# A decode kernel keeps part of a sixth record on chip between two rounds

## The chip, the cores and the metric

The kernel runs on one core of a Trainium2 chip. The metric is device time in microseconds (us), median of several runs. All data are 32-bit floats.

## What is computed

Four tokens (B = 4, D = 640) pass through two identical rounds. Each round is an attention over a cache and an MLP, both with a residual and a layer norm before them. The weights and the caches are the same in both rounds.

```python
# W = 1024 newest positions, Hq = 32 heads of Dh = 128, Dff = 1728
q = layernorm(x) @ wq                             # [4, 32, 128]
p = softmax(q . k_cache[:, :, -W:] * Dh ** -0.5)
x = x + (p . v_cache[:, :, -W:]) @ wo
h = relu(layernorm(x) @ w1)
x = x + h @ w2
# and all of it a second time
```

## The kernel before

**Records.** All that one head needs is packed in a record of 128 partitions by REC = 9,472 columns: the query weights (columns 0 to 640), K in two halves of 2,048 columns (640 to 4,736), V in two halves of 2,048 (4,736 to 8,832), and the output weights (8,832 to 9,472, from `WO`). A record is 4,736 KB. The MLP weights w1 (five chunks of FF = 1,728 columns) and w2 (54 tiles of FD = 160 columns) are 8,640 columns each. Per round, 32 records and both weights are read once; on-chip memory holds five whole records (`slot0` to `slot4`), a `ring` of 7,808 columns and, before the change, a tile `kept` of 1,152 columns.

**The order of the records.** Round zero goes through heads 0 to 31. The last five of them (27 to 31) stay in their slots, and round one begins with them, so that they are not loaded again; then it goes through 0 to 26. Of record 26, the last of round one, the columns from `KEPT` = 8,320 on stay in `kept` between the rounds.

**The loads.** All loads are in one list, `items`, written in the order in which they shall be issued. `pump()` walks the list strictly in order: it issues the first entry as soon as no column that it overwrites is `live`, and stops at the first that must wait. `done(key, lo, hi)` marks columns of a record as read and calls `pump()`. All loads are issued by SyncE (SP), in list order; at run time each waits for the readers of what it overwrites. Since one entry that must wait holds up all behind it, the list decides what the 16 DMA engines have queued.

**One head.** `query` multiplies the query weights by the normed input on PE (five matmuls into a PSUM tile, before the change `misc`), and DVE copies the result to `qT`. `scores` does 8 matmuls into one of two score tiles `sc_ps`, each of two PSUM banks. `softmax` takes the maximum on DVE and the exponentials on ACT in place. `weights` transposes them on DVE into `wT`. `values` does 8 matmuls into `o_ps`; `picks` and `output_T` bring the head's result into `oTs`, and `project` multiplies it by the output weights into `acc`. The heads are pipelined by hand: in iteration n of the main loop the scores of head n + 1, the values of head n and the query of head n + 2 are issued in this order.

**The end of a round.** The last three records are loaded in pieces (`ending`), so that the compute behind the last load is short. In round zero the output weights of the last five records come after them, then the MLP weights.

**The MLP of round zero.** At that time five slots hold records 27 to 31, so the 17,280 columns of MLP weights go through the ring (`MLP_RING`: name, size, first column in the ring). Before the change four chunks of w1 and five tiles of w2 fit at first; each later piece waits until the piece under it has been read. Behind the weights come the pieces of record 0 for round one, most of them into the ring too (`IN_RING`), the rest into the first slot that comes free (`IN_SLOT`). In round one the MLP weights go into slots that are free by then.

**Fillers.** `busy(n)` is a matmul whose result nobody reads; some are placed where PE would pause.

In the trace every operation stands at line 88 (L88), the helper `InOrder.call` that records them; the tiles' names tell them apart. The functions that the diff touches:

Of the kernel before, what the change touches and what calls it, by code (L numbers as in the profile page):

```python
# [32 lines left out]
F32 = mybir.dt.float32  # L33
AF = mybir.ActivationFunctionType
OP = mybir.AluOpType
# [3 lines left out]
P = 128  # L39
# [16 lines left out]
ENDS = 28  # L56
TILES[ENDS:ENDS] = [(13, 0), (13, 1)]
TCOLS = len(TILES) * FD
RING = 4 * FF + 896
KEPT = WO - 512  # L60

MLP_RING = [("w1", 1, 0), ("w1", 1, FF), ("w1", 1, 2 * FF), ("w1", 1, 3 * FF), ("w2", 5, 6912), ("w1", 1, 0),
            ("w2", 10, 1728), ("w2", 11, 3328), ("w2", 11, 5088), ("w2", 6, 6848), ("w2", 7, 0), ("w2", 4, 1120)]

IN_RING = [(256, 1664, 1760), (1664, 3200, 3168), (3200, 4736, 4704), (4736, 6272, 6240), (6272, 7296, 0),
           (7296, 7808, 1024)]

IN_SLOT = [(WO, REC, 0), (7808, WO, 640), (0, 256, 1664)]
W1_SLOT = [[0, 1], [2], [3], [4]]
W2_SLOT = [22, 20, 8, 4]  # L70
LATE = 5
# [24 lines left out]
def decode_kernel(ctx: ExitStack, tc: tile.TileContext, xf, rec, w1, w2, out):  # L96
# [5 lines left out]
    mean_of = sb.tile([P, P], F32, name="mean_of")  # L102
# [4 lines left out]
    x_sb = scratch[:, :FD]  # L107
    blocks = xT.rearrange("p (k j) -> p k j", j=32)[:, :, :B]
    spread = scratch[:, 256:288]
    hT = scratch.rearrange("p (m j) -> p m j", j=32)  # L110
# [12 lines left out]
    kept = sb.tile([P, REC - KEPT], F32, name="kept")  # L123
# [5 lines left out]
    misc = ps.tile([P, 512], F32, name="misc")  # L129
    outs = [o_ps, sc_ps[0][:, 512:]]  # L130

    dve.memset(x_sb, 0.0)
# [13 lines left out]
    dve.tensor_reduce(mean_of.rearrange("p (j s) -> p j s", j=NB), folded, op=OP.add, axis=AX.X)  # L146

    dve.tensor_reduce(of_block, mean_of[:, :16].rearrange("p (c j) -> p c j", j=4), op=OP.add, axis=AX.X)
    dve.tensor_reduce(pick, mean_of[:, :32].rearrange("p (c j) -> p j c", j=4), op=OP.add, axis=AX.X)
    dve.tensor_scalar(mean_of, mean_of, 1.0 / D, None, op0=OP.mult)  # L150
    dve.memset(small, EPS)
    dve.memset(eps_dh, EPS * DH)
    dve.memset(ones, 1.0)
# [1 line left out]
    for a in sc_ps:  # L155
        dve.memset(a, 0.0)

    order = [list(range(H)), list(range(H - NS, H)) + list(range(H - NS))]
    LAST = H - NS

    def home(h, r):

        return h % NS if not r or h >= LAST else (h - 6 + LAST) % NS

    items = []

    at = {("rec", 1, LAST - 1): [(KEPT, REC, "kept", 0)]}
    live = []
    buffers = dict(enumerate(slot)) | {"ring": ring, "kept": kept}

    def load(key, src, lo, hi, buf, col):
        items.append((key, src, lo, hi, buf, col))
# [16 lines left out]
    piece(0, hs[0], 0, V)  # L189
    piece(0, hs[0], V, REC)  # L190
    for h in hs[1:-3]:
        piece(0, h, 0, KEPT if h == LAST - 1 else WO if h >= H - LATE else REC)
        if h == LAST - 1:
            piece(0, h, KEPT, REC, "kept", 0)
    ending(0, hs, True)
    loaded = {"w1": 0, "w2": 0}
    for name, size, col in MLP_RING:
# [1 line left out]
        load((name, 0), {"w1": w1, "w2": w2}[name], n, loaded[name], "ring", col)  # L199


    hs = order[1]
    old = [home(h, 0) for h in hs[:NS]]
    new = hs[NS:]
    for lo, hi, col in IN_RING:
        piece(1, new[0], lo, hi, "ring", col)
    for lo, hi, col in IN_SLOT:
        piece(1, new[0], lo, hi, old[0], col)
    piece(1, new[1], K + VH, V, old[0], K + VH)
    piece(1, new[1], 0, K + VH, old[1], 0)  # L210
    piece(1, new[1], V, V + VH, old[1], K + VH)
    piece(1, new[1], V + VH, REC, old[0], V)
    for i in range(2, 6):
        piece(1, new[i], 0, V, *((old[i], 0) if i < 5 else ("ring", 0)))
        piece(1, new[i], V, REC, old[i - 1], V)
    for h in new[6:-3]:
        piece(1, h, 0, REC)
    ending(1, hs, False)
    for ks in W1_SLOT:
        load(("w1", 1), w1, ks[0] * FF, (ks[-1] + 1) * FF, home(LAST + 1, 0), ks[0] * FF)  # L220
    n = 0
    for size in W2_SLOT:
        load(("w2", 1), w2, n * FD, (n + size) * FD, home(LAST + 2, 0), n * FD)
        n += size

    def pump():

        while items:
            key, src, lo, hi, buf, col = items[0]
            if any(b == buf and x < col + hi - lo and col < y for b, x, y in live):  # L230
# [3 lines left out]
            at.setdefault(key, []).append((lo, hi, buf, col))  # L234
            items.pop(0)

    def pieces(key):
# [2 lines left out]
    def cols(key, lo, n):  # L240
# [3 lines left out]
                return buffers[buf][:, col + lo - x:col + lo - x + n]  # L244
        raise KeyError((key, lo, n))

    def done(key, lo, hi):

        if key[0] == "rec" and key[1] == 0 and key[2] >= LAST:
            return  # L250
        for x, y, buf, col in pieces(key):
            a, b = col + max(lo, x) - x, col + min(hi, y) - x
            if a < b:
                rest = []
                for bb, u, v in live:
                    if bb != buf or v <= a or b <= u:
                        rest.append((bb, u, v))
                    else:
                        rest += [(bb, p, q) for p, q in ((u, a), (b, v)) if p < q]
                live[:] = rest  # L260
        pump()


    def busy(n, to=sc_ps[1]):

        pe.matmul(to[0:1, :n], mean_of[:, 0:1], slot[home(LAST, 0)][:, K:K + n], start=True, stop=True)

    def center(fill):

        x = acc[:, :FD]  # L270
        dve.tensor_reduce(sums, x, op=OP.add, axis=AX.X)
        if fill:
            busy(256)
        pe.matmul(misc[:, :B], sums.to_broadcast([P, P]), pick, start=True, stop=True)
        dve.transpose(xT, x)
        dve.scalar_tensor_tensor(blocks, misc[:, :B].unsqueeze(1).to_broadcast([P, KB, B]), -1.0 / D, blocks,
                                 op0=OP.mult, op1=OP.add)
        dve.tensor_tensor(spread[:, :KB * B].rearrange("p (k b) -> p k b", b=B), blocks, blocks, op=OP.mult)
        dve.tensor_reduce(squares, spread[:, :KB * B].rearrange("p (k b) -> p b k", b=B), op=OP.add, axis=AX.X)
# [75 lines left out]
    def mlp(r):  # L355
# [39 lines left out]
    for r in range(2):  # L395
        hs = order[r]
        late = LATE if r == 0 else 2
        center(r > 0)
        query(r, hs[0])
        scores(r, hs[0], 0, True)  # L400
        softmax(0, True)
        query(r, hs[1])
# [71 lines left out]
```

## Time and profile before

| | |
|---|---|
| runs (us) | 718.20, 717.31, 719.21; median 718.2 |
| span of the profiled execution (first to last instruction) | 715.0 us; its own time was not listed beside it, only the three runs |
| busy share of the span | PE 73%, DVE 50%, PE weight loads 30%, ACT 13% |
| DMA | 303.90 MB, mean 425 GB/s |
| HBM | read 303.25 MB, written 0.08 MB |

The page has six parts: busy time by engine; the span in 40 slices, each digit a busy share in tenths; the DMA queues with their share of 16 engines' span; the chain of work that ended last, followed back from the last instruction; the costliest groups of instructions; and the DMA issues with the median time from issue to landing. A load lands when the last of the 16 DMA engines has finished its part. An issue early in its queue has a long time to landing without costing anything: the time is that of the loads ahead of it.

### The profile page before, as it was taken

The page shows a single profiled execution, that of the slowest core. Times are in us where ns is not written, and L with a number is a line of the kernel's source. Part 1 is how long each engine was busy: PE and PEld are TensorE (multiplying, and loading weights), DVE is VectorE, ACT ScalarE, POOL GpSimd, SP SyncE. Part 2 cuts the span into 40 slices and gives each one's busy share as a digit, 9 for nine tenths or more (in the row PEclk, how much of TensorE's full clock was granted, in tenths as well). Part 3 has the DMA queues.
Part 4 walks back from the last instruction along what each step waited for, and adds up shares of the span by engine and source line. Part 5 has one row for each costly group of instructions (what it writes and reads, how often), then busy time and mean ns, then how long its engine had stood idle before and what let it go on. Part 6 is the DMA issues. An engine that isn't in the chain of part 4 may idle for free.

```text
span 715.0 us, 8905 instructions
## 1 busy us (share of the span) xinstructions
PE 523.8 (73%) x3694; PEld 212.8 (30%) x3694; DVE 357.8 (50%) x1010; ACT 93.1 (13%) x145; POOL 1.1 (0%) x9
## 2 busy tenths in 40 slices
PE   4465868676677776759889898876877777586867
PEld 2131323322223231323224333332332323232323
DVE  3354535454444544446731777744444444455751
ACT  1201011010101101011110211201010110101201
POOL 0000000000000000000000000000000000000000
PEclk9678767668866868777999999957576677868989
DMA  9999999999999999999999999999999999999996
GB/s 374 439 438 433 422 435 435 439 432 420 438 440 433 425 429 439 427 428 429 426 415 390 426 426 433 441 430 427 435 441 429 433 425 438 437 429 422 432 423 290
DMA packets 15913, 303.90 MB, mean 425 GB/s; under 512 B 1777, under 2 KB 2049, under 8 KB 6145
## 3 DMA queue, kind: packets, MB, share of 16 engines
q1 hardware_dynamic: 15840, 303.32, 99.1%
q8 instruction: 29, 0.48, 0.2%
q14 instruction: 12, 0.09, 0.0%
q10 hardware_dynamic: 32, 0.01, 0.0%
HBM read 303.25 MB, written 0.08 MB: 424 GB/s over the span
## 4 chain that ended last, share of the span: by engine, by line
DMA 76%; PE 19%; DVE 4%; issue 1%; another core or an unknown queue 1%; ACT 0%
DMA slot<-rec 73%; PE sc_ps L88 7%; PE misc L88 5%; PE o_ps L88 4%; PE acc L88 3%; DMA ring<-w 3%; DVE scratch L88 2%; DVE small L88 1%; DVE oTs L88 1%; DVE t_ps L88 0%; ACT sc_ps L88 0%; DVE xT L88 0%; DVE qT L88 0%; DVE mrt L88 0%
## 5 line engine op out<-in xcount | busy, mean ns | idle before, releaser
L88 PE MATMUL misc<-xT,slot 128*128 128x4 f32 x624 | 103.3, 292 | 146.3 <-DMA slot<-rec 145.8
L88 PE MATMUL sc_ps<-slot,qT 128*4 128x512 f32 x992 | 199.0, 943 | 1.5 <-DVE qT L88 1.3
L88 PEld LDWEIGHTS misc<-xT,slot 128*128 128x128 f32 x624 | 97.7, 242 | 203.2 <-DMA slot<-rec 190.9
L88 ACT ACTIVATE sc_ps<-sc_ps,small 128x1024 f32<-128x1024 f32 (+1 forms) x68 | 76.7, 1127 | 552.2 <-DVE small L88 551.2
L88 PE MATMUL o_ps<-slot,scratch 128*16 128x512 f32 x978 | 137.5, 679 | 4.0 <-DVE scratch L88 2.6
L88 DVE TENSOR_REDUCE small<-sc_ps 128x1 f32<-128x1024 f32 x64 | 78.3, 1223 | 78.1 <-PE sc_ps L88 78.1
L88 DVE STREAM_TRANSPOSE t_ps<-sc_ps 128x512 f32<-128x512 f32 x128 | 93.2, 728 | 2.1
L88 DVE COPY qT<-misc 128x4 f32<-128x4 f32 x64 | 10.2, 160 | 158.1 <-PE misc L88 158.1
L88 PEld LDWEIGHTS o_ps<-slot,scratch 128*16 128x16 f32 x978 | 33.6, 119 | 132.8 <-issue 82.5
L88 DVE SCALAR_TENSOR_TENSOR scratch<-o_ps,of_block,scratch 128x128 f32<-128x128 f32 x186 | 65.2, 351 | 6.6
L88 PEld LDWEIGHTS sc_ps<-slot,qT 128*4 128x4 f32 x992 | 33.1, 115 | 83.8 <-issue 73.1
L88 PE MATMUL acc<-slot,oTs 128*4 128x160 f32 x496 | 36.9, 382 | 16.1 <-DVE oTs L88 15.6
L88 DVE TENSOR_SCALAR scratch<-o_ps,of_block 128x128 f32<-128x128 f32 x62 | 21.7, 350 | 35.4 <-PE o_ps L88 35.4
L88 PE MATMUL o_ps<-pick,scratch 128*128 128x4 f32 x124 | 28.8, 303 | 5.8 <-DVE scratch L88 5.8
L88 DVE TENSOR_TENSOR scratch<-t_ps,mrt 128x64 f32<-128x64 f32 x128 | 28.8, 225 | 4.7
L88 PEld LDWEIGHTS o_ps<-pick,scratch 128*128 128x128 f32 x124 | 25.8, 256 | 8.6 <-DVE scratch L88 8.6
L88 DVE COPY oTs<-o_ps 128x4 f32<-128x4 f32 x62 | 10.0, 162 | 14.1 <-PE o_ps L88 12.9
L88 PE MATMUL sc_ps<-slot,mean_of 128*1 128x512 f32 (+1 forms) x36 | 16.8, 558 | 0.0
L88 DVE TENSOR_SCALAR mrt<-of_batch,small 128x4 f32<-128x4 f32 x64 | 14.7, 230 | 2.2
L88 DVE STREAM_TRANSPOSE scratch<-small 128x32 f32<-128x32 f32 x64 | 12.9, 202 | 2.4 <-ACT sc_ps L88 2.4
L88 PEld LDWEIGHTS acc<-slot,oTs 128*4 128x4 f32 x496 | 6.8, 84 | 22.1 <-DVE oTs L88 20.8
L88 ACT ACTIVATION_READ_ACCUMULATOR sc_ps<-sc_ps,small 128x1 f32 x64 | 12.2, 191 | 0.0
(69 smaller groups left out, 119.4 us busy)
## 6 DMA issues: line engine op xcount, KB each, us to landing
slot<-rec SPq DMA_DIRECT2D x43, 4736.0 KB, 30.8
slot<-rec SPq DMA_DIRECT2D x17, 2368.0 KB, 18.8
slot<-rec SPq DMA_DIRECT2D x2, 4416.0 KB
slot<-rec SPq DMA_DIRECT2D x5, 1024.0 KB, 30.4
ring<-w SPq DMA_DIRECT2D x5, 864.0 KB, 10.8
slot<-rec SPq DMA_DIRECT2D x1, 4160.0 KB, 34.5
slot<-rec SPq DMA_DIRECT2D x2, 2048.0 KB, 42.0
slot<-rec SPq DMA_DIRECT2D x2, 1344.0 KB, 9.2
```

Source lines behind the costliest of these rows:

```text
L88: r = build(*args, **kwargs)
```

## The change

Record 26 (`SIXTH`) gets a home of its own, the ring, which grows from 7,808 to 9,152 columns; `kept` and `mean_of` go. In round zero it is loaded there as columns 0 to 9,152; its last 320 columns are loaded later over the first 320 of the ring, whose query weights have been read by then. After round zero has used the record, its columns from `HELD` = 5,024 on stay. The 320 columns and columns 5,024 to 5,216 are copied by DVE (`put_by`) into `hold`, a PSUM bank of 512 columns. That leaves the first `KEPT` = 5,216 columns of the ring for the MLP weights of round zero, and behind them for columns 0 to 5,024 of record 26, which are loaded again (`SIXTH_PIECES`). In round one record 26 comes sixth, after 27 to 31, and after its query DVE copies the 512 columns back (`put_back`). The other records of round one go whole into the slots, and w1 of round one goes into the ring.

To make a bank free, `misc` goes: queries are now written to the first four columns of the score tile that the same head's scores will fill next, and the small matmul of `center` to `o_ps`. Fillers take `ones` in place of `mean_of`, those in `values` write to `sc_ps[0]`, and in round one's MLP the three fillers behind the middle w1 chunks go.

```diff
-RING = 4 * FF + 896
-KEPT = WO - 512
-
-MLP_RING = [("w1", 1, 0), ("w1", 1, FF), ("w1", 1, 2 * FF), ("w1", 1, 3 * FF), ("w2", 5, 6912), ("w1", 1, 0),
-            ("w2", 10, 1728), ("w2", 11, 3328), ("w2", 11, 5088), ("w2", 6, 6848), ("w2", 7, 0), ("w2", 4, 1120)]
-
-IN_RING = [(256, 1664, 1760), (1664, 3200, 3168), (3200, 4736, 4704), (4736, 6272, 6240), (6272, 7296, 0),
-           (7296, 7808, 1024)]
-
-IN_SLOT = [(WO, REC, 0), (7808, WO, 640), (0, 256, 1664)]
+SIXTH = H - NS - 1
+RING = WO + 2 * FD
+KEPT = 3 * FF + 32
+HELD = KEPT - 192
+
+MLP_RING = [("w1", 1, 0), ("w1", 1, FF), ("w1", 1, 2 * FF), ("w1", 1, 0), ("w1", 1, FF), ("w2", 11, 2 * FF),
+            ("w2", 10, 0), ("w2", 10, FF), ("w2", 11, 2 * FF), ("w2", 10, 0), ("w2", 2, FF)]
+
+SIXTH_PIECES = [(2048, 2 * FF), (2 * FF, HELD), (0, FF), (FF, 2048)]
...
-    order = [list(range(H)), list(range(H - NS, H)) + list(range(H - NS))]
     LAST = H - NS
+    order = [list(range(H)), list(range(LAST, H)) + [SIXTH] + list(range(SIXTH))]
 
     def home(h, r):
 
-        return h % NS if not r or h >= LAST else (h - 6 + LAST) % NS
+        if h == SIXTH:
+            return "ring"
+        return h % NS if not r or h >= LAST else (h + LAST) % NS
...
-    at = {("rec", 1, LAST - 1): [(KEPT, REC, "kept", 0)]}
+    at = {("rec", 1, SIXTH): [(0, RING, "ring", 0), (RING, REC, "ring", 0)]}
...
-        last = WO if late else KEPT
-        for h, lo, hi in ((a, 0, V), (b, 0, V), (a, V, end), (c, 0, V), (b, V, end), (c, V, V + VH), (c, V + VH, last)):
+        for h, lo, hi in ((a, 0, V), (b, 0, V), (a, V, end), (c, 0, V), (b, V, end), (c, V, V + VH), (c, V + VH, end)):
...
-        piece(0, h, 0, KEPT if h == LAST - 1 else WO if h >= H - LATE else REC)
-        if h == LAST - 1:
-            piece(0, h, KEPT, REC, "kept", 0)
+        piece(0, h, 0, RING if h == SIXTH else WO if h >= H - LATE else REC)
+    piece(0, SIXTH, RING, REC, "ring", 0)
     ending(0, hs, True)
...
+    for lo, hi in SIXTH_PIECES:
+        load(None, rec[SIXTH], lo, hi, "ring", lo)
+    new = order[1][NS + 1:]
+    for i, lo, hi in ((0, 0, K), (0, K, K + VH), (0, K + VH, V), (1, 0, K + VH), (1, K + VH, V), (0, V, V + VH),
+                      (0, V + VH, REC), (2, 0, V), (1, V, REC), (3, 0, V), (2, V, REC), (4, 0, V), (3, V, REC),
+                      (4, V, REC)):
+        piece(1, new[i], lo, hi)
...
+    ending(1, new, False)
     for ks in W1_SLOT:
-        load(("w1", 1), w1, ks[0] * FF, (ks[-1] + 1) * FF, home(LAST + 1, 0), ks[0] * FF)
+        load(("w1", 1), w1, ks[0] * FF, (ks[-1] + 1) * FF, "ring", ks[0] * FF)
...
-        load(("w2", 1), w2, n * FD, (n + size) * FD, home(LAST + 2, 0), n * FD)
+        load(("w2", 1), w2, n * FD, (n + size) * FD, home(new[-5], 1), n * FD)
...
+        if key == ("rec", 0, SIXTH):
+            hi = min(hi, HELD)
...
+    held = [(0, 0, REC - RING), (REC - RING, HELD, KEPT)]
+
+    def put_by():
+
+        for col, a, b in held:
+            dve.tensor_copy(hold[:, col:col + b - a], ring[:, a:b])
+            free("ring", a, b)
+        pump()
+
+    def put_back():
+
+        for col, a, b in held:
...
+            dve.tensor_copy(ring[:, a:b], hold[:, col:col + b - a])
+            live.append(("ring", a, b))
...
-        pe.matmul(to[0:1, :n], mean_of[:, 0:1], slot[home(LAST, 0)][:, K:K + n], start=True, stop=True)
+        pe.matmul(to[0:1, :n], ones, slot[home(LAST, 0)][:, K:K + n], start=True, stop=True)
...
-    def query(r, h):
+    def query(r, h, s):
+        q = sc_ps[s][:, :B]
         key = ("rec", r, h)
         for k in range(KB):
-            pe.matmul(misc[:, 8:8 + B], cols(key, WQ + k * DH, DH), xblock(k), start=(k == 0), stop=(k == KB - 1))
+            pe.matmul(q, cols(key, WQ + k * DH, DH), xblock(k), start=(k == 0), stop=(k == KB - 1))
         done(key, WQ, K)
-        dve.tensor_copy(qT, misc[:, 8:8 + B])
+        dve.tensor_copy(qT, q)
...
-                busy(512, misc)
+                busy(512, sc_ps[0])
...
-            elif k < KB - 1:
+            elif r == 0 and k < KB - 1:
                 busy(512)
...
-            query(r, hs[n + 2])
+            query(r, hs[n + 2], n % 2)
...
+            if r == 0 and h == SIXTH:
+                put_by()
+            if r == 1 and hs[n + 2] == SIXTH:
+                put_back()
```

More of the change, by code (lines that the diff above doesn't have):

```diff
@@ L100, in decode_kernel @@
     ps = ctx.enter_context(tc.tile_pool(name="ps", bufs=1, space=PSUM))
-    mean_of = sb.tile([P, P], F32, name="mean_of")
     xT = sb.tile([P, FD], F32, name="xT")
@@ L107, in decode_kernel @@
     x_sb = scratch[:, :FD]
+    same = scratch[:, FD:FD + P]
     blocks = xT.rearrange("p (k j) -> p k j", j=32)[:, :, :B]
@@ L122, in decode_kernel @@
     ring = sb.tile([P, RING], F32, name="ring")
-    kept = sb.tile([P, REC - KEPT], F32, name="kept")
     sc_ps = [ps.tile([P, W], F32, name=f"sc_ps{i}") for i in range(2)]
@@ L128, in decode_kernel @@
     acc = ps.tile([P, 512], F32, name="acc")
-    misc = ps.tile([P, 512], F32, name="misc")
+    hold = ps.tile([P, 512], F32, name="hold")
     outs = [o_ps, sc_ps[0][:, 512:]]
@@ L145, in decode_kernel @@
     folded = ident.rearrange("p (j s) -> p s j", j=NB).unsqueeze(1).to_broadcast([P, NB, 32, NB])
[L146 to L150, printed above, removed]
+    dve.tensor_reduce(same.rearrange("p (j s) -> p j s", j=NB), folded, op=OP.add, axis=AX.X)
+    dve.tensor_reduce(of_block, same[:, :16].rearrange("p (c j) -> p c j", j=4), op=OP.add, axis=AX.X)
+    dve.tensor_reduce(pick, same[:, :32].rearrange("p (c j) -> p j c", j=4), op=OP.add, axis=AX.X)
     dve.memset(small, EPS)
@@ L156, in decode_kernel @@
         dve.memset(a, 0.0)
-    order = [list(range(H)), list(range(H - NS, H)) + list(range(H - NS))]
     LAST = H - NS
+    order = [list(range(H)), list(range(LAST, H)) + [SIXTH] + list(range(SIXTH))]
     def home(h, r):
-        return h % NS if not r or h >= LAST else (h - 6 + LAST) % NS
+        if h == SIXTH:
+            return "ring"
+        return h % NS if not r or h >= LAST else (h + LAST) % NS
     items = []
-    at = {("rec", 1, LAST - 1): [(KEPT, REC, "kept", 0)]}
+    at = {("rec", 1, SIXTH): [(0, RING, "ring", 0), (RING, REC, "ring", 0)]}
     live = []
-    buffers = dict(enumerate(slot)) | {"ring": ring, "kept": kept}
+    buffers = dict(enumerate(slot)) | {"ring": ring}
     def load(key, src, lo, hi, buf, col):
@@ L199, in decode_kernel @@
         load((name, 0), {"w1": w1, "w2": w2}[name], n, loaded[name], "ring", col)
[L202 to L216, printed above, removed]
+    for lo, hi in SIXTH_PIECES:
[5 more added lines that the diff above has]
+        piece(1, new[i], lo, hi)
+    for h in new[NS:-3]:
         piece(1, h, 0, REC)
-    ending(1, hs, False)
+    ending(1, new, False)
     for ks in W1_SLOT:
-        load(("w1", 1), w1, ks[0] * FF, (ks[-1] + 1) * FF, home(LAST + 1, 0), ks[0] * FF)
+        load(("w1", 1), w1, ks[0] * FF, (ks[-1] + 1) * FF, "ring", ks[0] * FF)
     n = 0
     for size in W2_SLOT:
-        load(("w2", 1), w2, n * FD, (n + size) * FD, home(LAST + 2, 0), n * FD)
+        load(("w2", 1), w2, n * FD, (n + size) * FD, home(new[-5], 1), n * FD)
         n += size
@@ L233, in pump @@
             live.append((buf, col, col + hi - lo))
-            at.setdefault(key, []).append((lo, hi, buf, col))
+            if key:
+                at.setdefault(key, []).append((lo, hi, buf, col))
             items.pop(0)
@@ L245, in cols, with free @@
         raise KeyError((key, lo, n))
+    def free(buf, a, b):
+        rest = []
+        for bb, u, v in live:
+            if bb != buf or v <= a or b <= u:
+                rest.append((bb, u, v))
+            else:
+                rest += [(bb, p, q) for p, q in ((u, a), (b, v)) if p < q]
+        live[:] = rest
     def done(key, lo, hi):
@@ L253, in done @@
             if a < b:
[L254 to L260, printed above, removed]
-        pump()
+                free(buf, a, b)
+        pump()
+    held = [(0, 0, REC - RING), (REC - RING, HELD, KEPT)]
[6 more added lines that the diff above has]
+        for col, a, b in held:
+            assert not any(buf == "ring" and x < b and a < y for buf, x, y in live), (a, b, live)
+            dve.tensor_copy(ring[:, a:b], hold[:, col:col + b - a])
+            live.append(("ring", a, b))
     def busy(n, to=sc_ps[1]):
-        pe.matmul(to[0:1, :n], mean_of[:, 0:1], slot[home(LAST, 0)][:, K:K + n], start=True, stop=True)
+        pe.matmul(to[0:1, :n], ones, slot[home(LAST, 0)][:, K:K + n], start=True, stop=True)
     def center(fill):
@@ L273, in center @@
             busy(256)
-        pe.matmul(misc[:, :B], sums.to_broadcast([P, P]), pick, start=True, stop=True)
+        pe.matmul(o_ps[:, :B], sums.to_broadcast([P, P]), pick, start=True, stop=True)
         dve.transpose(xT, x)
-        dve.scalar_tensor_tensor(blocks, misc[:, :B].unsqueeze(1).to_broadcast([P, KB, B]), -1.0 / D, blocks,
+        dve.scalar_tensor_tensor(blocks, o_ps[:, :B].unsqueeze(1).to_broadcast([P, KB, B]), -1.0 / D, blocks,
                                  op0=OP.mult, op1=OP.add)
@@ L398, in decode_kernel @@
         center(r > 0)
-        query(r, hs[0])
+        query(r, hs[0], 0)
         scores(r, hs[0], 0, True)
         softmax(0, True)
-        query(r, hs[1])
+        query(r, hs[1], 1)
         weights(0)
```

## The prediction

> **What bounds the kernel now.** I read the page first: span, the row of DMA tenths, the queues, the chain that ended last.
>
> ```profile
> span 715.0 us, 8905 instructions
> DMA  9999999999999999999999999999999999999996
> GB/s 374 439 438 433 422 435 435 439 432 420 438 440 433 425 429 439 427 428 429 426 415 390 426 426 433 441 430 427 435 441 429 433 425 438 437 429 422 432 423 290
> q1 hardware_dynamic: 15840, 303.32, 99.1%
> DMA 76%; PE 19%; DVE 4%; issue 1%; another core or an unknown queue 1%; ACT 0%
> ```
>
> Loads fill the 16 DMA engines for 99.1% of the span, from the first slice to the last but one. No slice is idle; the 22nd (375 to 393 us), where round zero's MLP runs out of the ring and round one begins, is the slowest of the inner ones at 390 GB/s. The chain says the same: 76% of it is a DMA.
>
> Then the windows view, for the rate of an undisturbed stretch and of that stage (columns: stretch, length, busy time and count on PE, PEld, DVE, ACT, POOL, granted clock, DMA share, GB/s), and the waits of a late stretch (446 to 680 us), for how far the compute is from binding:
>
> ```profile
> 374.00:388.00 14.00, 12.96 (x149) 5.58 (x141) 1.63 (x5) 1.08 (x3) 0.00 (x0) 1.00 0.99 380
> 500.00:650.00 150.00, 110.64 (x704) 46.15 (x708) 72.31 (x202) 16.85 (x26) 0.00 (x0) 0.72 1.00 432
> PE misc L88 <- DMA slot<-rec: 51.6, 18, 4.3
> ```
>
> Undisturbed, a load moves 432 GB/s. A column (128 partitions of four bytes) is 512 bytes, so 1,000 columns cost 1.185 us. PE waits for the next record 18 times, 2.9 us on average: up to that much extra compute in each record of this stretch is free.
>
> The end, from the chain and from SP's timeline (the third row holds the last two loads, issued at 689.07 and about 690.9), with the issue row of the last load (320 KB, 20.6 us from issue to landing):
>
> ```profile
> 681.02 2.30 PE misc L88 x10
> 707.75 4.26 PE acc L88 x112
> 712.03 0.33 DVE scratch L88
> 689.07 2.15 SPq L88 DMA_DIRECT2D slot<-w  x2
> slot<-w SPq DMA_DIRECT2D x1, 320.0 KB, 20.6
> ```
>
> The last weights land at 690.9 + 20.6 = 711.5, the last matmuls on them end at 712.0 and the copy out at 712.4. The compute that starts with the K half of the last record (681.0) arrives at that same moment. So two things tie at the end: the sum of all loads, and the 31 us of compute behind the last record's K half.
>
> **The bytes removed.** Before, round one loads 27 records less the 1,152 columns in `kept`: 27 x 9,472 - 1,152 = 254,592. After, it loads 26 records and, of record 26, only the 5,024 columns up to HELD: 26 x 9,472 + 5,024 = 251,296. Round zero and the weights are unchanged. That is 3,296 columns, 1.69 MB; at 1.185 us per 1,000 it is **-3.9 us** of a queue that never rests. Four issues fewer (105 against 109) I cost at nothing: SP's 0.33 us each lies beside the transfers.
>
> **The end still follows the loads.** After, the last record's tail is loaded whole, so 4,736 + 2,048 + 2,688 + 17,280 = 26,752 columns come behind its K half (the other half of the record before, its own two value pieces, the weights), where 25,600 did. The compute behind it therefore gets 1,152 columns, 1.4 us, more room, and three of round one's MLP fillers leave PE's queue, each at least as long as its pace in this timeline, 0.43 us (the second starts 0.43 us after the first; they come in two passes):
>
> ```profile
> 701.55 0.59 PE L88 MATMUL sc_ps<-slot,mean_of 128*1 128x512 f32 x1
> 701.98 0.59 PE L88 MATMUL sc_ps<-slot,mean_of 128*1 128x512 f32 x1
> ```
>
> Of the tie only the loads remain, and the 0.9 us from the last landing to the copy's end stays. So the compute adds nothing and takes nothing away: 0.
>
> **The smaller ring.** This is the price. The MLP weights of round zero went through 7,808 columns and now go through 5,216, that is 2,592 columns or 3.1 us less of loads queued ahead; behind them record 0 filled 7,552 columns and record 26 now fills 5,024, 3.0 us less. Is there that much to spare? SP's timeline gives three refill issues; the issue rows give their time to landing, each asked for by itself, and that of two later ones:
>
> ```profile
> 371.10 0.33 SPq L88 DMA_DIRECT2D ring<-w  x1
> ring<-w SPq DMA_DIRECT2D x1, 800.0 KB, 7.5
> 373.50 0.33 SPq L88 DMA_DIRECT2D ring<-w  x1
> ring<-w SPq DMA_DIRECT2D x1, 880.0 KB, 7.2
> 375.09 0.33 SPq L88 DMA_DIRECT2D ring<-w  x1
> ring<-w SPq DMA_DIRECT2D x1, 880.0 KB, 7.7
> 387.12 0.38 SPq L88 DMA_DIRECT2D ring<-rec  x1
> ring<-rec SPq DMA_DIRECT2D x1, 256.0 KB, 9.5
> ring<-w SPq DMA_DIRECT2D x1, 480.0 KB, 4.5
> ```
>
> First, the dip to 380 GB/s is not yet a stall of the path: the three land at 378.6, 380.7 and 382.8, 2.1 us apart for 880 KB, which is full rate. Landings follow the slowest of the 16 engines; only faster ones ran dry. Second, the spare: 7.2 to 7.7 us less 3.1 leaves 4.1 to 4.6 from issue to landing, of which the transfer takes 1.9 to 2.1. What is left, 2.2 to 2.5 us, must hold the fixed part of a load (issue, first byte, receipt). The trace never shows that part alone. It is at least nothing; at most, from the 480 KB row, 4.5 less 1.1 of transfer, 3.4 us; the nearest row is the output, 80 KB from the copy's end at 712.4 to the end of the span at 715.0, 2.6 us less 0.2 of transfer and with the program's end in it. I take 2.4.
>
> So refills fit to within 0.2 us, and what they miss counts once per turn of the ring: three chunks are 5,184 columns, 12,096 columns of weights and the 5,024 of record 26 are refilled, 3.3 turns. By 0 the cost is 0, by 2.4 it is 0 to 0.7 us, by 3.4 it is 1.2 x 3.3 = 4.0 us. I take **+0.3 us**.
>
> The Trainium skill, page "DMA: Bandwidth & Descriptors", section "Anatomy of one DMA — SWDGE (gpsimd) path", gives a load a fixed part of about 2.0 us beside its bytes, for another issuing engine than SP; by that figure every refill still fits, the cost is 0 and the time 714.3 us, as an estimate. No row here shows that part alone, so the sum keeps its own bounds.
>
> At the start of round one the ring's last piece landed at 387.12 + 9.5 = 396.6; 3.0 us earlier is 393.6. Then comes record 0's query part (640 columns, 0.8 us, released by the query of record 27) until 394.4, and then the first K half, released by these scores:
>
> ```profile
> 389.66 1.89 PE sc_ps L88 x8
> ```
>
> They end at 391.6; with 2.4 us the queue is fed at 394.0, 0.4 us in time; by 3.4 it is 0.6 us late. Cost 0, at worst 0.6.
>
> **The sixth record and SP's queue.** Record 26's last 320 columns wait for its own query (they overwrite it), and SP issues in order, so records 29 to 31 wait behind that. Whole records are issued far ahead:
>
> ```profile
> slot<-rec SPq DMA_DIRECT2D x43, 4736.0 KB, 30.8
> ```
>
> Of 30.8 us about 11.2 are the transfer, some 20 us are queue; 27 and 28 stand in it when the query of 26 runs, so this delay, about one record, is covered. If that cover were gone it would cost up to 11 us. The weights in the ring then wait for `put_by`, which runs in 26's own iteration, over two records ahead of their turn: 0.
>
> **The four copies.** DVE's rows by form:
>
> ```profile
> L88 DVE COPY qT<-misc 128x4 f32<-128x4 f32 x64 | 10.2, 160 | 158.1 <-PE misc L88 158.1
> L88 DVE COPY scratch<-acc 128x160 f32<-128x160 f32 x1 | 0.3, 326 | 3.9 <-PE acc L88 3.9
> ```
>
> From 160 ns for 4 columns and 326 for 160 comes 1.06 ns a column: 0.50 us for 320 columns, 0.36 for 192, 0.86 us for each of `put_by` and `put_back` (the rows copy out of PSUM, one of these goes into it; from nothing to twice that would change no conclusion). `put_by` stands before the next maximum on DVE, in a stretch where PE waits 2.9 us per record. `put_back` stands in the compute-bound start of round one and delays one record by 0.9 us; loads are then queued ahead, in `slot` pieces like this, issued at 424.9:
>
> ```profile
> slot<-rec SPq DMA_DIRECT2D x1, 2368.0 KB, 19.1
> ```
>
> 19.1 us with 5.6 of transfer: 13 us ahead. Less the 3 us and the 0.9 it remains fed. 0.
>
> **`misc` gives up its bank.** Queries now write the first four columns of the score tile that is next to be filled. Its old scores were read by the transposes of the iteration before, and `values`, ahead of the query on PE, already waits for these. New scores there already wait for the copy to `qT`. So no wait is added; were one, up to 2.9 us a record would be hidden. `mean_of` for `ones` in the fillers changes no shape. 0.
>
> **Sum.** -3.9 + 0.3 = -3.6 us: the profiled 715.0 becomes 711.4. The runs' median, 718.2, lies 3.2 above the profiled span, for launch and end, which stay: **714.6 us**. About 0.3%, 2.2 us, is what this kernel's measurement tells from no change (three runs span 717.3 to 719.2).
>
> **Rivals.** *Starved refills.* The fixed part is nearer 3.4 us, and the ring turns 3.3 times with 1.2 us of waiting each, perhaps half of that: 1.5 to 4 us of the gain go, 716 to 718. For it: the margin is near 0, and the stage's dip shows that some engines already run dry. Against: landings kept full pace.
> *Slower: PE at half clock through the weights.* The trace grants half clock in places; here a w1 chunk lasts longer than at full clock:
>
> ```profile
> 367.54 0.91 PE sc_ps L88 x8
> 369.41 1.62 PE L88 MATMUL sc_ps<-ring,xT 128*4 128x432 f32 x8 [0.65 <-DMA ring<-w]
> 370.81 1.06 PE L88 MATMUL sc_ps<-slot,mean_of 128*1 128x512 f32 x1
> ```
>
> If all five chunks fall into such a stretch, each with such a filler behind it, a chunk costs 2.7 us where its load takes 2.05: 3.2 us late, and with it the refills, up to 4.0: -3.9 + 7.2 = +3.3, 721 us. It decides from 6.1 us lost on. Against: the stretch from 374 to 388 had a clock of 1.00.
> *No fewer bytes on the path:* the end is compute after all and the loads saved become idle time. Time 718.2. Against: the compute behind the last K half starts 4,448 columns, 5.3 us, earlier.
>
> **How the numbers follow.** Forecast 0.70 (713.0 to 716.0, faster). Starved refills 0.19 (0.08 still faster by over 0.3%, 0.11 within it). Half clock with starved refills 0.07, slower. Bytes off the path 0.04, within. Faster 0.78, within 0.3% 0.15, slower 0.07. The range: below, no stall and a scatter of a microsecond as the runs show, 713.0; above, half of the starved case, 717.0; what lies outside is the slower rival and the rest of the starved one and of the fourth, under 0.2.
>
> **What would show it.** q1 moves 1.69 MB less, 301.6 MB; its share stays at about 99%; the stretch from 366 to 396 us shows refills with 4 to 5 us from issue to landing and no landing gap over the transfer; the last w2 lands 3 to 4 us earlier and the copy out 0.9 us behind it. Wrong would be: DMA share visibly under 0.9 between 368 and 396; SP waiting for the query of 26 with an empty queue behind it; a PE wait for w2 at the end longer than before.

## The result and the profile after

The change makes no difference that can be measured: 718.55 us (median of 12 runs) against 718.38 before, a ratio of 1.0006 with a 95% interval from 0.9991 to 1.0022. Measured a second time, on another chip, it was 1.0006 [0.9985, 1.0026]. The forecast was 714.6.

The page of the kernel after (span, DMA share and GB/s in 40 slices of 17.9 us, the load queue, the chain that ended last):

```profile
span 717.1 us, 8939 instructions
DMA  9999999999999999999989999999999999999996
GB/s 377 435 435 434 435 428 430 436 434 433 430 430 434 435 432 435 431 427 424 424 345 333 409 434 428 444 425 434 436 433 436 422 431 436 438 434 418 429 426 286
q1 hardware_dynamic: 15264, 301.64, 98.6%
DMA 80%; PE 15%; DVE 3%; issue 1%; another core or an unknown queue 0%; DVEq 0%; SPq 0%
```

The bytes went as planned: 303.32 MB became 301.64. Yet the span is longer, and the queue's share fell from 99.1% to 98.6%. Most of that stands in two slices, the 21st and 22nd (359 to 394 us), with 345 and 333 GB/s where before had 415 and 390. The windows view of the last head of round zero (354 to 361) and of the MLP with the start of round one (366 to 398); columns as in the prediction, the last three are granted clock, DMA share and GB/s. Before, then after:

```profile
354.00:361.00 7.00, 5.25 (x39) 0.89 (x32) 5.61 (x14) 1.30 (x2) 0.00 (x0) 1.00 0.99 411
366.00:398.00 32.00, 27.55 (x235) 10.83 (x234) 6.89 (x28) 5.73 (x10) 0.00 (x0) 0.89 1.01 400
```

```profile
354.00:361.00 7.00, 6.06 (x36) 1.02 (x25) 5.25 (x14) 1.29 (x2) 0.00 (x0) 0.52 0.99 412
366.00:398.00 32.00, 24.75 (x240) 9.52 (x240) 5.67 (x23) 4.44 (x8) 0.00 (x0) 0.96 0.90 324
```

In 32 us the change moves 76 GB/s less, 2.43 MB; at 432 GB/s that is 5.6 us, more than the 3.9 us of bytes that it saves. The waits of 366 to 400 us name who stands still (engine, tile, releaser: us in total, times, longest). Before, then after:

```profile
PEld sc_ps L88 <- DMA ring<-w: 2.4, 2, 1.7
PE sc_ps L88 <- DMA ring<-w: 2.4, 3, 1.0
PEld acc L88 <- DMA ring<-w: 0.5, 1, 0.5
```

```profile
PEld acc L87 <- DMA ring<-w: 6.4, 4, 2.1
PEld sc_ps L87 <- DMA ring<-w: 5.6, 3, 3.4
PE sc_ps L87 <- DMA ring<-w: 3.0, 2, 2.5
PE acc L87 <- DMA ring<-w: 2.7, 4, 1.2
```

PE now waits for the ring all through the MLP. The timeline of after shows the loop, PE's reads and SP's issues (SP's third row is the first slot that comes free in round one):

```profile
368.68 0.91 PE L87 MATMUL sc_ps<-ring,xT 128*4 128x432 f32 x8 [0.80 <-DVE sc_ps L87]
369.65 16.14 SPq L87 DMA_DIRECT2D ring<-w  x8
...
375.68 0.91 PE L87 MATMUL sc_ps<-ring,xT 128*4 128x432 f32 x8 [2.51 <-DMA ring<-w]
377.94 0.91 PE L87 MATMUL sc_ps<-ring,xT 128*4 128x432 f32 x8 [0.52 <-DMA ring<-w]
...
382.79 0.99 PE L87 MATMUL acc<-ring,scratch 128*4 128x160 f32 x20 [0.79 <-DMA ring<-w]
386.04 5.72 SPq L87 DMA_DIRECT2D ring<-rec  x4
388.01 0.86 PE L87 MATMUL acc<-ring,scratch 128*4 128x160 f32 x19 [1.18 <-DMA ring<-w]
393.44 3.51 SPq L87 DMA_DIRECT2D slot<-rec  x3
```

The first chunk is read from 368.68 to 369.6, and only then, at 369.65, can the first refill be issued. The three chunks that the ring holds have all landed by 371.3 in the trace. The refill is read at 375.68, 6.0 us after its issue; at full pace it would have landed 2.05 us (its transfer) behind the third chunk, at 373.3. The DMA slices of 366 to 400 us (0.85 us each) show the hole; before, then after:

```profile
DMA  9999999999999989989999999999999999999999
```

```profile
DMA  9755396999999999979999989999989958989999
```

There are two holes: at 367 to 372, and at 392 to 394, where the first pieces of record 26 come. The end itself is as before, with the copy out right behind the last matmuls on the last weights (713.64, waiting for the DMA):

```profile
713.64 0.11 PEld L87 LDWEIGHTS acc<-slot,scratch 128*4 128x4 f32 x8 [0.35 <-DMA slot<-w]
714.16 0.33 DVE L87 COPY scratch<-acc 128x160 f32<-128x160 f32 x1 [4.29 <-PE acc L87]
```

### The profile page after: what moved, and what is told of

Its sections match the earlier page's. It is cut to its first block, busy times and chain, and to the rows that moved or that the text cites. A ratio compares the mean times of both kernels' runs of the same rounds, so it can differ in the third digit from the quotient of the medians.

```text
span 717.1 us, 8939 instructions
## 1 busy us (share of the span) xinstructions
PE 516.8 (72%) x3686; PEld 208.9 (29%) x3686; DVE 359.1 (50%) x1013; ACT 93.0 (13%) x145; POOL 1.1 (0%) x9
## 3 DMA queue, kind: packets, MB, share of 16 engines
q1 hardware_dynamic: 15264, 301.64, 98.6%
## 4 chain that ended last, share of the span: by engine, by line
DMA 80%; PE 15%; DVE 3%; issue 1%; another core or an unknown queue 0%; DVEq 0%; SPq 0%
DMA slot<-rec 68%; PE sc_ps L87 8%; DMA ring<-rec 6%; PE o_ps L87 4%; DMA slot<-w 3%; PE acc L87 3%; DMA ring<-w 3%; DVE scratch L87 2%; DVE oTs L87 1%; DVE small L87 0%; DVE t_ps L87 0%; DVE ring L87 0%; DVE mrt L87 0%; DVE xT L87 0%
## 5 line engine op out<-in xcount | busy, mean ns | idle before, releaser
L87 PE MATMUL sc_ps<-xT,slot 128*128 128x4 f32 x620 | 99.5, 287 | 148.9 <-DMA slot<-rec 146.6
L87 PEld LDWEIGHTS sc_ps<-xT,slot 128*128 128x128 f32 x620 | 95.4, 238 | 203.7 <-issue 194.0
L87 PE MATMUL o_ps<-slot,scratch 128*16 128x512 f32 x960 | 132.9, 674 | 2.5 <-DVE scratch L87 1.6
L87 DVE COPY qT<-sc_ps 128x4 f32<-128x4 f32 x64 | 10.2, 160 | 160.9 <-PE sc_ps L87 160.9
L87 PE MATMUL sc_ps<-slot,small 128*1 128x512 f32 (+1 forms) x36 | 17.1, 568 | 0.0
L87 DVE COPY oTs<-o_ps 128x4 f32<-128x4 f32 x62 | 10.0, 162 | 14.0 <-PE o_ps L87 12.9
L87 DVE STREAM_TRANSPOSE scratch<-small 128x32 f32<-128x32 f32 x64 | 12.9, 202 | 1.6 <-ACT sc_ps L87 1.6
L87 PE MATMUL sc_ps<-ring,xT 128*4 128x432 f32 x80 | 10.0, 605 | 4.6 <-DMA ring<-w 3.0
```

The lines of the kernel that those rows point to most:

```text
L87: r = build(*args, **kwargs)
```

## The experiments

**Theories.** A: what runs ahead is too short. The ring's free part fell from 7,808 to 5,216 columns, and at two places, the start of the MLP and the start of round one, the queue runs dry while SP waits for PE; that gives back what the bytes save. B: the delay of PE, which worked at half clock in the last head, is what costs, whatever the ring. T: the end of the kernel gains or loses something that the prediction put at nothing.

**The yardstick.** Two quantities are worked out from every trace. The loss in the MLP is the time from the landing of the first w1 chunk of round zero to that of the last w2 piece, less the columns that land between, at 1.185 us per 1,000. The loss at the start of round one is the same from there to the landing of the first half record that is loaded in one piece (2,368 KB, at some 415 to 427 us).

**1. Four chunks in the ring.** Part of record 26 is given back to the loads: 1,728 columns more to load than the change, 1,568 fewer than before.

```diff
-KEPT = 3 * FF + 32
+KEPT = 4 * FF + 32
...
+MLP_RING = [("w1", 1, 0), ("w1", 1, FF), ("w1", 1, 2 * FF), ("w1", 1, 3 * FF), ("w1", 1, 0), ("w2", 10, FF),
+            ("w2", 10, 2 * FF), ("w2", 11, 3 * FF), ("w2", 10, 0), ("w2", 10, FF), ("w2", 3, 2 * FF)]
...
+SIXTH_PIECES = [(2 * FF + 480, 3 * FF), (3 * FF, HELD), (0, FF), (FF, 2 * FF), (2 * FF, 2 * FF + 480)]
```

> The change with a ring of 6,944 columns for the weights (four chunks, not three) and so 6,752 columns of record 26 loaded again (not 5,024). Theory A, the ring is too shallow: what the change saves in bytes it loses again while the DMA engines run dry at the start of round zero's MLP and at the start of round one; 1,728 columns more depth cover 2.0 us of each gap, 1,728 columns more to load cost 2.0 us once, so the net is a gain over the change: 717.2 to 718.0, 0.3 to 1.0 us under the kernel before. Theory B, the loss comes from another part of the change (queries in the score banks, fillers, copies): the depth does nothing and the bytes cost 2.0 us, 720 to 721.

Measured: 714.79 us, 0.9957 [0.9942, 0.9971]: faster than both kernels, by more than was expected. The stage is whole again:

```profile
366.00:398.00 32.00, 27.05 (x232) 9.75 (x232) 6.42 (x26) 5.73 (x10) 0.00 (x0) 0.89 1.01 397
```

**2. Four chunks, without reloading the extra part.** Bytes as in the change, ring as in experiment 1; columns 5,024 to 6,752 of record 26 are not loaded again (the edit is against experiment 1).

```diff
-SIXTH_PIECES = [(2 * FF + 480, 3 * FF), (3 * FF, HELD), (0, FF), (FF, 2 * FF), (2 * FF, 2 * FF + 480)]
+SIXTH_PIECES = [(2 * FF + 480, 5024), (0, FF), (FF, 2 * FF), (2 * FF, 2 * FF + 480)]
```

> As four_chunks, but columns 5,024 to 6,752 of record 26 are not loaded again (left out), so that it loads as many bytes as the change with a ring one chunk deeper in the MLP; the depth at the start of round one is that of the change. Theory A: the gap at the start of the MLP closes, 2 to 3 us; the gap at the start of round one stays: 715.5 to 716.5. Theory B: no difference from the change, 718 to 719.

Measured: 715.63 us, 0.9963 [0.9946, 0.998]. With the change's bytes and one chunk more of ring the time is 2.9 us better than the change: that is the hole in the MLP (loss 0.6 us where the change has 4.7). But 2.05 us of loads fewer than in experiment 1 make nothing faster: at the start of round one the loss is 4.3 us, against 2.0 there. The bytes left out there only make the second hole longer.

**3 and 4. 3.2 us of DVE work that PE waits for**, before round zero's MLP, in the kernel before and in the change.

```diff
+        if r == 0:
+            for _ in range(4):
+                dve.transpose(t_ps, sc_ps[1][:, 512:])
+            dve.tensor_copy(xT, xT)
```

> The kernel before with 3.2 us of DVE work between round zero's last norm and its MLP, so that the ring is read 3.2 us later. Theory A: the old ring holds 7.1 us of loads behind the first chunk and lets DMA run on; 0.5 to 1.5 us slower. Theory B (depth does not matter, loads are late for another reason): as much slower as late_after is against the change.

> The change with the same 3.2 us of DVE work before round zero's MLP. Theory A: its ring is already empty when the MLP starts, so that the whole delay comes through: 3.0 to 3.3 us slower than the change, about 721.7. Theory B: the same cost as in late_before.

Measured: 721.35 us, 1.0052 [1.0032, 1.0073], and 722.75 us, 1.0057 [1.0039, 1.0075]. The second is 3.7 to 4.2 us over the change, somewhat more than expected; the first, 3.0 to 3.7 us over before, is a miss for A, as the old ring pays the delay nearly as the new one does. In both traces the delay is longer than the DVE work: PE came out of it with a clock of 0.50 and read the first chunk in 1.62 us instead of 0.91, so that the first refill was issued 4.4 and 4.2 us later than in the traces of before and of the change. How much of that the old ring could take is read from the trace of before. Its first refill is issued alone, by the end of the first chunk's matmuls,

```profile
368.51 0.33 SPq L88 DMA_DIRECT2D ring<-w  x1
```

and what was queued lands at 374.5, so that the refill's place at full pace is at 374.5 + 2.05 = 376.55. The delayed change shows what a load takes on an empty queue; its DMA slices and GB/s from 366 to 400 us, then SP's issue and PE's read of that load:

```profile
DMA  9854300000869999958999999999999899898999
GB/s 407 342 236 195 138 41 0 0 0 0 114 252 407 390 376 407 238 207 331 375 395 414 444 384 380 383 389 429 379 361 256 348 415 267 325 359 322 380 407 389
```

```profile
373.81 4.14 SPq L87 DMA_DIRECT2D ring<-w  x3
378.35 0.11 PEld L87 LDWEIGHTS sc_ps<-ring,xT 128*4 128x4 f32 x8 [0.88 <-DMA ring<-w]
```

Nothing moves from 371.1 to 374.5; 864 KB issued at 373.81 are read at 378.35, 4.5 us later, of which 2.05 are the transfer. So before's first refill would arrive at 368.51 + 4.5 = 373.0 on an empty queue, 3.5 us ahead of its place. The delay of 4.4 us goes past that by 0.9, and the refill of the delayed kernel landed 1.0 us behind its place. The rest of its loss in the MLP, 4.9 us in all, comes with the later refills, which start from there. (Its profile, 725.8 us, is its slowest run.)

**5. The fillers alone**: the kernel before without the three fillers of round one's MLP.

```diff
-            elif k < KB - 1:
+            elif r == 0 and k < KB - 1:
```

> The kernel before without the three fillers of round one's MLP, the one edit of the change that touches the compute behind the last load. Theory T (in the kernel before, compute and loads tie at the end, and where half clock falls on the last MLP the compute ends later): 0.5 to 1.3 us faster, 717.1 to 717.9. Theory L (the end follows the loads alone): no difference.

Measured: 717.11 us, 0.9993 [0.9981, 1.0006]. The interval holds the gain that T forecast and none at all; not resolved.

**6. The banks alone**: the kernel before with queries in the score banks, `center` on `o_ps` and `ones` in the fillers.

```diff
...
-            pe.matmul(misc[:, 8:8 + B], cols(key, WQ + k * DH, DH), xblock(k), start=(k == 0), stop=(k == KB - 1))
+            pe.matmul(q, cols(key, WQ + k * DH, DH), xblock(k), start=(k == 0), stop=(k == KB - 1))
...
```

> The kernel before with the queries written into the score banks, center's matmul into o_ps and fillers from ones, the ring and the loads as they were. If these edits are free, as predicted: within 0.15% of the kernel before. If a shared bank adds a wait that loads do not hide: slower by over 0.3%, which would then be part of what the change lost.

Measured: 717.37 us, 1.0001 [0.9986, 1.0017]: free, to within 0.2%. Its profile shows something else. Windows of 700 to 709 us, before and then this kernel, and this kernel's end:

```profile
700.00:709.00 9.00, 9.00 (x95) 3.25 (x88) 1.35 (x5) 2.65 (x5) 0.00 (x0) 1.00 0.93 392
```

```profile
700.00:709.00 9.00, 9.00 (x48) 2.04 (x49) 0.48 (x3) 1.58 (x2) 0.00 (x0) 0.69 0.87 367
```

```profile
710.43 4.07 PE L88 MATMUL acc<-slot,scratch 128*4 128x160 f32 x112
...
714.59 0.33 DVE L88 COPY scratch<-acc 128x160 f32<-128x160 f32 x1 [3.47 <-PE acc L88]
```

The last load lands at 711.44 in the trace, as before (711.5), yet the copy out comes at 714.59 instead of 712.03: here the compute ends 2.6 us late. PE had a clock of 0.69 in round one's MLP, where before had 1.00; that this is the whole reason was not tested. Of the other traces with the old end, those of before and of experiment 5 don't show it, that of experiment 3 does (2.4 us). In all ten traces of kernels with the sixth record the copy is 0.56 or 0.57 us behind the last landing.

**7. Two chunks**, the dose upward: 1,728 columns fewer to load than the change, one chunk less of ring.

```diff
-KEPT = 3 * FF + 32
+KEPT = 2 * FF + 32
...
+MLP_RING = [("w1", 1, 0), ("w1", 1, FF), ("w1", 1, 0), ("w1", 1, FF), ("w1", 1, 0), ("w2", 11, FF),
+            ("w2", 10, 0), ("w2", 11, FF), ("w2", 10, 0), ("w2", 11, FF), ("w2", 1, 0)]
...
+SIXTH_PIECES = [(160, FF), (FF, HELD), (0, 160)]
```

> The change with a ring of 3,488 columns for the weights (two chunks) and 3,296 columns of record 26 loaded again: 1,728 columns (2.0 us) fewer to load than in the change, and as many fewer ahead. Theory A, depth: in both gaps DMA runs dry 2.0 us sooner, and each refill of the weights waits for a whole turn, some 4.5 us for a chunk on an empty queue and 1 us to read it, for two chunks 5.5 us against 4.1 of transfer: 722 to 728. Bytes alone: 716.5.

Measured: 724.32 us (4 runs), 1.0087 [1.0061, 1.0114], as A has it. Fewer bytes, more time:

```profile
366.00:398.00 32.00, 20.52 (x192) 7.86 (x196) 3.40 (x16) 2.66 (x5) 0.00 (x0) 0.95 0.85 287
```

**8. Four chunks with the three fillers of round one's MLP**, as before the change (the edit is against experiment 1).

```diff
-            elif r == 0 and k < KB - 1:
+            elif k < KB - 1:
```

> four_chunks with the three fillers of round one's MLP put back. Theory T, with the longer stretch of loads behind the last K half still giving 1.4 us of room: 0 to 0.7 us slower than four_chunks, 714.8 to 715.5. If the fillers were all of the extra gain: 716.

Measured: 715.56 us, 0.9964 [0.9949, 0.998]; against 0.9957 and 0.9950 without them the intervals overlap. Fillers are not what made experiment 1 better than expected.

**9 and 10. The change and four chunks again**, on one chip.

> The change once more, unedited, beside the others on one chip and for a second profile. The first profile read the first weight chunk 2.5 us after it landed, 1.4 us later than before, since PE had half clock in the last head of round zero. If the loss is the depth of the ring, it comes without that too: ratio to the kernel before within 0.998 to 1.003, and again 2 us or more lost by landings between the third and fourth chunk or later refills. If it was that stretch of half clock, this profile, if free of it, shows 2 to 4 us less span.

> four_chunks once more, unedited, beside the change on one chip. Theory A: 0.994 to 0.997 of the kernel before, so that four chunks are 2 to 4 us faster than three.

Measured: 719.40 us, 1.0006 [0.9985, 1.0026], and 715.58 us, 0.9950 [0.9931, 0.9969]. The change's second profile has the same stage:

```profile
366.00:398.00 32.00, 25.80 (x238) 9.46 (x237) 5.14 (x21) 4.44 (x8) 0.00 (x0) 0.90 0.92 338
```

**11. The change, with its held part loaded again too**: 3,936 columns, 4.7 us of transfer, right behind the pieces of record 26.

```diff
-SIXTH_PIECES = [(2048, 2 * FF), (2 * FF, HELD), (0, FF), (FF, 2048)]
+SIXTH_PIECES = [(2048, 2 * FF), (2 * FF, HELD), (0, FF), (FF, 2048), (KEPT, RING)]
...
+        free("ring", KEPT, RING)
```

> The change, but columns 5,216 to 9,152 of record 26, which stand in the ring all the time, are loaded again behind the other pieces of record 26: 3,936 columns, 4.7 us, more to load, and so much more queued at the start of round one; the MLP's ring is as in the change. If the gap at the start of round one is real (2 to 2.5 us) that part comes back: 2 to 3 us slower than the change, 720.5 to 721.5. If only the MLP's gap exists: 4.7 us slower, 723.

Measured: 721.50 us, 1.0040 [1.0023, 1.0057]. Of 4.7 us of transfer only 0.34%, 2.4 us, appear in the time. The other 2.2 us (by the medians of 9 and 11, 2.6) fill time in which the change's queue stands idle. In the traces a part of that is at the start of round one: from the landing of the ring's last piece of record 26 to that of the first half record, the change loses another 0.9 and 3.3 us, this kernel 0.6. The rest may lie in the MLP, where this trace lost less than those of the change, for a reason that comes below.

**12. Five chunks**: 160 columns more to load than before, a ring 864 columns larger.

```diff
-KEPT = 3 * FF + 32
+KEPT = 5 * FF + 32
...
+MLP_RING = [("w1", 1, 0), ("w1", 1, FF), ("w1", 1, 2 * FF), ("w1", 1, 3 * FF), ("w1", 1, 4 * FF), ("w2", 10, 0),
+            ("w2", 10, FF), ("w2", 10, 2 * FF), ("w2", 10, 3 * FF), ("w2", 11, 4 * FF), ("w2", 3, 0)]
...
+SIXTH_PIECES = [(480, FF), (FF, 2 * FF), (2 * FF, 3 * FF), (3 * FF, 4 * FF), (4 * FF, HELD), (0, 480)]
```

> The change with a ring of 8,672 columns for the weights (all of w1 at once) and 8,480 columns of record 26 loaded again, 160 columns more bytes than the kernel before. Theory A: no gap is left to close, so against four_chunks only the bytes count, 1,728 columns, 2.0 us slower: 716.5 to 717.5, four chunks being next to the best. If depth still pays at four: at or below four_chunks, 715.

Measured: 716.53 us, 0.9977 [0.9963, 0.9991]. All 12 runs lie between 716.47 and 716.78; those of before and of the change spread over 4 us and more, those of four chunks over 2. In the stage:

```profile
366.00:398.00 32.00, 27.89 (x250) 9.64 (x248) 9.12 (x31) 5.73 (x10) 0.00 (x0) 0.95 1.02 421
```

This run closes the account. With five chunks hardly anything starves, so its 716.5 us less 1.185 us per 1,000 columns is what a kernel would take by its bytes; what its profiled execution took beyond that should be its losses beyond those of five chunks (0.3 in the MLP and 1.3 behind it). A time is longer than the span of its execution by 2.0 us for before (median of its 92 later runs, 1.7 to 2.2) and by 1.7 for kernels with the sixth record, so that before's profiled execution took about 717.0. All in us:

| kernel | ring | by bytes | profiled execution | beyond | loss MLP | loss start | sum less 1.6 |
|---|---|---|---|---|---|---|---|
| five chunks | 8,672 | 716.5 | 716.5 | 0 | 0.3 | 1.3 | 0 |
| before | 7,808 | 716.3 | 717.0 (715.0 + 2.0) | 0.7 | 0.4 | 1.6 | 0.4 |
| before, no fillers | 7,808 | 716.3 | 718.8 | 2.5 | 1.0 | 3.0 | 2.4 |
| before, banks | 7,808 | 716.3 | 719.3 | 3.0 | 0.3 | 1.4 | 0.0, and 2.6 at the end |
| four chunks (1, 10) | 6,944 | 714.4 | 714.8, 714.5 | 0.4, 0.1 | 1.0, 0.4 | 2.0, 1.1 | 1.4, -0.2 |
| four, not reloaded | 6,944 | 712.4 | 715.1 | 2.7 | 0.6 | 4.3 | 3.3 |
| the change (first, 9) | 5,216 | 712.4 | 718.8, 720.1 | 6.4, 7.7 | 4.7, 3.8 | 3.0, 5.7 | 6.1, 7.8 |
| the change, reloaded | 5,216 | 717.0 | 721.1 | 4.1 | 3.0 | 2.9 | 4.2 |
| two chunks | 3,488 | 710.3 | 723.2 | 12.9 | 8.1 | 5.9 | 12.3 |
| the change, PE late | 5,216 | 712.4 | 723.5 | 11.1 | 8.1 | 5.2 | 11.7 |
| before, PE late | 7,808 | 716.3 | 725.8 | 9.5 | 4.9 | 3.0 | 6.3, and 2.4 at the end |

The columns "beyond" and "sum less 1.6" agree within about 1 us in every row, losses at the end included. So by this account the change's bytes would bring it to 712.4, and the two holes put back 6 to 8 us. The net is nothing because before loses too: its median of 718.4 is 2.1 above its bytes. That the two cancel so closely is a coincidence of this ring size. Four chunks is the best of the rings tried, 0.4 to 0.6% under both kernels.

B holds in part. Both profiles of the change had a clock of 0.52 in the last head and issued the first refill at 369.6; it landed 2.3 and 2.0 us behind its place at full pace. The reloaded change, with the same ring, had 1.00 there and issued it at 368.05. Three rows of its trace, the issue, PE's read of that refill, and the read before which PE waits longest:

```profile
368.05 0.33 SPq L87 DMA_DIRECT2D ring<-w  x1
373.31 0.91 PE L87 MATMUL sc_ps<-ring,xT 128*4 128x432 f32 x8 [0.41 <-DMA ring<-w]
385.99 0.86 PE L87 MATMUL acc<-ring,scratch 128*4 128x160 f32 x19 [1.97 <-DMA ring<-w]
```

Here the first refill is only 0.1 us behind its place (landed at 373.26, against 371.11 + 2.05 = 373.16), and yet the MLP loses 3.0 us, nearly all of it with later refills; the largest single loss, 1.7 us, is the one that lands at 385.94. So by these three traces half clock makes some 1 to 2 us of the hole, and depth the rest. No run takes the clock alone.

## Why the prediction was wrong, step by step

- **The bytes** (-3.9 us): right, 301.64 MB and, by the table, 716.3 less 3.9.
- **The smaller ring** (+0.3 us): here it failed. By the traces it is 4.3 and 3.3 us in the MLP beyond before's 0.4, and 2.5 in the reloaded change, which had full clock in the last head. The spare was read from the refills at 371.10, 373.50 and 375.09, which stand behind others in a queue that has not run out, and a refill was taken to need its transfer and a fixed part of 2.4 us and no more, 4.3 to 4.5 us. (Row by row, what is left for the fixed part is 2.0 to 2.5 us, not 2.2 to 2.5.) The change's refills took 6.0 to 7.6 us from issue to landing, those of the reloaded change 5.2 to 6.6. Their issue also hangs on PE: a piece is reloaded only when it has been read, and read only when it has landed, so that a load that comes late makes the next one late. The sum that was missing is that of a whole turn: a load on an empty queue and its reading take 4.5 + 1.0 = 5.5 us, two chunks of transfer cover 4.1, three 6.1, four 8.2. Two chunks ran at 5.6 us a turn through w1, as this gives. Three leave 0.6 us, which the refills' longer times more than use up; four leave 2.7. What makes up these longer times was not taken apart: the parts of one load, on 16 engines, ended 0.8 to 2.4 us apart, and PE pauses between w1 and w2.
- **The fixed part of a load** (2.4 us): right. Experiment 4 gives 4.5 - 2.05 = 2.5 us. The Trainium skill, page "DMA: Bandwidth & Descriptors", section "Anatomy of one DMA — SWDGE (gpsimd) path", has about 2.0 us for another issuing engine; for SP the measured 2.5 decides. With either, the change's first refill, issued at 369.65, is late: it should land by 373.3.
- **The start of round one** (0, at worst 0.6): wrong, 1.7 and 4.4 us over five chunks in the two profiles. The reckoning took the pieces of record 26 to land 3.0 us earlier than those of record 0. But they go into the ring behind w2 tiles that PE now reads late: the second was issued at 389.04, and the ring's last piece landed at 398.4, where 393.6 was reckoned and before had 396.6. The scores that were to end at 391.6 and release the next load began only at 393.66.
- **The end** (0): right for the profiled execution, where it still follows the loads. It leaves out a gain in other executions: in two of four traces with the old end the compute made it 2.4 and 2.6 us later (in experiment 6 at a clock of 0.69), in none of the ten with the sixth record. What that is worth on average the runs don't settle; experiment 5, which takes the fillers alone, gives -0.5 us with an interval from -1.4 to 0.4.
- **From the profiled execution to the median** (+3.2 us): not a constant. Of it 2.0 us are the way from the span to the time, which is 0.3 us shorter with the sixth record (1.7; why, no run shows). The profiled execution of before took about 717.0 us, and 38 of its 92 later runs took under 717.3; the remaining 1.2 us were losses that its slower runs had and this one had not. A profile better than the median hid how near the edge the ring was.
- **Banks, copies, SP's order** (0): the banks are right by experiment 6; copies and order show no cost in five chunks, whose time is that of the best runs of before (716.5).
- **The rivals.** Starved refills (716 to 718) named what happened, with the wrong reason, a fixed part of 3.4 us, and too low a price, 4.0 us at most. Half clock came, in the head ahead of the weights and not through them.
- **What was to show it.** Refills were to take 4 to 5 us without a gap; they took 6.0 to 7.6 (4.8 for the last, 160 KB). The last w2 was to land 3 to 4 us earlier; it landed at 713.6, 2.1 later.

## What to carry to other kernels

On-chip space that keeps data resident is taken from space that lets loads run ahead, and between the two there was an optimum: here the ring at 3,488, 5,216, 6,944 and 8,672 columns gave 1.0087, 1.0006, 0.9950 to 0.9957 and 0.9977. To price a shallower queue, don't take a refill from the steady flow. Find the first one after each point where the loads wait for compute, and compare its issue plus a load's time on an empty queue with the landing of what is queued ahead plus its own transfer. Then compare the transfers of a whole turn with a load's time plus its reading, and leave room for refills that take longer. Look also at how far the runs spread: the kernel here that hardly starves repeats within 0.3 us, and a spread of several us says that the profile at hand may be a lucky one.

## What the runs showed of the hardware

- A load that SP issues on an empty queue takes 2.5 us beyond its transfer (864 KB in 4.5 us, in experiment 4).
- The 16 DMA engines drift apart: the parts of one load ended 2.1 us apart at 375.6 in the change and up to 4 us apart before a stall, and a load counts by its last part. So slices fall below nine tenths while the landings still keep full pace, as at the ring of before.
- The change got a clock of 0.52 in the last head (354 to 361 us) in both profiles, the reloaded change, which differs only in what follows, 1.00. In the twelve traces without added delay the first refill follows that clock: 369.6 at 0.52, 369.0 to 369.3 at 0.77 and 0.78, 368.05 to 368.5 at 1.00. That the runs of before and of the change spread by 4 us fits this; what sets the clock's phase was not tested.
